# Seven block products in place of eight in the last first product of a mixer layer

## The chip, the core and the metric

One core of one Trainium2 chip runs the whole kernel as one program. The metric is the device time of one execution in microseconds. Five engines with queues of their own work side by side: PE (matrix products), DVE and ACT (elementwise work), POOL, and SP, which here only issues transfers. Each takes its instructions strictly in the order of its queue and waits there for what the instruction needs.

## What is computed

Attention inside clusters, then a channel mixing layer, then a token and channel mixer. Only the end of the last step is touched:

```python
def _moe2_ref(x, w_tok1, w_tok2, w_ch1, w_ch2):      # x: (2, 768, 512)
    xt = x.transpose(0, 2, 1)
    h = np.maximum(xt @ w_tok1, 0.0) @ w_tok2
    u = x + h.transpose(0, 2, 1)
    h2 = np.maximum(u @ w_ch1, 0.0) @ w_ch2          # w_ch1: (512, 1536), w_ch2: (1536, 512)
    return (u + h2).astype(np.float32)
```

The two products of `h2` are done one batch after the other; the change is in the first product (`u @ w_ch1`) of the second batch.

## The kernel before

**Numbers.** The weights lie in DRAM as 64-bit floats. A unit is 512 KB of them: 128 columns of `w_ch1` (all 512 rows) or 128 rows of `w_ch2`. `w_issue` (L440) starts its load into one of five staging places (`ring`); `w_split` (L450) turns it into a high and a low float32 part with five operations on DVE and two on ACT. Activations are split into the same two parts, and each product is three passes (`PASSES`): high × high, low × high, high × low.

**Units.** `c1` and `c2` are the 12 units each of the last layer. There are 14 places for converted units. `seq` is the order of loads: after the 24 units for the first batch it loads ten of them again (`CH_RELOAD`: units 4 to 0 of both kinds), since their places are given to later units in the first batch, and they are converted a second time for the second batch.

**The layer.** `ff` (L1316) goes over the 12 units of one batch. For each it does the first product in two halves of 384 rows (L1332: 4 blocks of 128 contracted channels × 3 passes = 12 matmuls of 384 columns each, into one of two PSUM banks "x" and "m"), which `act_relu` empties: ACT takes the high part (L1311), DVE the low part (L1313). Then comes the second product of the unit before (L1356: six tiles of 128 rows × 3 passes = 18 matmuls of 512 columns, summed over all units in six PSUM banks). After the last unit `finish` (L1505) adds the six banks to the input on DVE (L1508), and SP sends each out (L1509). The first batch goes through units 0 to 11, the second through 11 to 0.

**The turned input.** `Turned` (L1422) brings `u` of one batch into the form with channels on partitions: six transposes on DVE (L1437), 16 transfers on SP and POOL (L1454) and eight splits (`part`: ACT L1465, DVE L1467). `ut0` is that of the first batch, `ut1` that of the second.

**What sets the order.** The program is written out by a small planner: work on DVE, ACT and SP is made of `Chain`s, whose steps are put into the engines' queues in the order of planned times; among steps that could start within a short window the one with the earlier `due` goes first. PE's matmuls are written out by the code itself; `after` and `claim` make it wait for a chain. `later` holds chains that begin when a condition is met.

Of the kernel before, what the change touches and what calls it, by code (L numbers as in the profile page):

```python
# [9 lines left out]
F32 = mybir.dt.float32  # L10
# [293 lines left out]
def cluster_attention_moe_mixer(ctx: ExitStack, tc, q, k, v, cent, mu_k, mu_r, w_k, w_v, w_r, w1, w2, wc1, wc2, out):  # L304
# [9 lines left out]
    stk = ctx.enter_context(tc.tile_pool(name="stk", bufs=2))  # L314

# [30 lines left out]
    now = {"P": 0.0, "A": 0.0, "D": 0.0, "G": 0.0, "S": 0.0, "N": 0.0}  # L346
# [3 lines left out]
    class Chain:  # L350
# [14 lines left out]
        def step(self, n=1):  # L365
            for _ in range(n):
# [7 lines left out]
                self.ready = t + LAT  # L374
# [37 lines left out]
    units, slot_of, free_slots, staged = {}, {}, [], []  # L412
    ring = [(stg, f"raw{i}") for i in range(NSTG)]
# [8 lines left out]
    for i in range(NFC):  # L422
        seq += [("c1", i), ("c2", i)]
    for i in CH_RELOAD:
        seq += [("c1", i), ("c2", i)]
# [24 lines left out]
    def w_split():  # L450
# [5 lines left out]
        def gen():  # L456
# [16 lines left out]
            if dense[0] and seq:  # L473
                w_issue()
# [9 lines left out]
            )  # L484

# [5 lines left out]

    active, due = [], {}

    def feed():
        while staged and free_slots and staged[0][0] not in units and sum(not c.done for c in active) < 2:
            w_split()
        for wait in list(later):
# [759 lines left out]
    for n, i in enumerate(CH_RELOAD):  # L1257
        again["c1", i] = ff2 + FB * (NFC + CH_KEEP + n)
        again["c2", i] = again["c1", i] + 0.75 * FB
# [57 lines left out]
    def ff(order, ka, kb, xin, square, dropped):  # L1317
        accs, prev, chains, rls = [], None, [], []
        nf = len(order)
        for idx in range(nf + 1):  # L1320
            cur = None
            if idx < nf:
# [22 lines left out]
                cur = hl  # L1345
            if prev is not None:
                f = order[idx - 1]
                u = need((kb, f))
                for ch in chains[:2]:
# [72 lines left out]
    class Turned:  # L1422


        def __init__(self, x2, before, due):
            self.x2, self.t, self.ch, self.before, self.due = x2, None, {}, before, due
            self.added, self.main = {}, None
# [4 lines left out]
        def gen(self):  # L1432
# [12 lines left out]
            for hf in range(2):  # L1445
                for c in range(KD):
                    self.ch[hf, c] = Chain(self.part(hf, c), self.due + 4 * hf + c, now["S"] + MOVE_US)
# [11 lines left out]
        def part(self, hf, c):  # L1459
# [3 lines left out]
            src = self.u[:, :, 3 * hf : 3 * hf + 3, c, :].rearrange("p q t r -> p t q r")  # L1463
# [41 lines left out]
    def finish(b, x2, accs):  # L1505
# [5 lines left out]
        for st in range(NT):  # L1511
            banks[st] = Chain(add(st), 0.0, now["P"] + 0.2), 1

# [28 lines left out]
    ut1 = Turned(s1.x2, None, ff2 + NFC * FB - 20)  # L1542
    later.append((lambda adds=adds: all_done(adds)() and ut0.whole(), ut1.begin))
    a0 = ff(list(range(NFC)), "c1", "c2", ut0, False, CH_RELOAD)
    due.update({k: t for k, t in again.items() if k[0] in ("c1", "c2")})
    finish(0, s0.x2, a0)
    a1 = ff(list(range(NFC - 1, -1, -1)), "c1", "c2", ut1, False, list(range(NFC)))
# [38 lines left out]
```

## Time and profile before

| | us |
|---|---|
| median of 3 runs | 617.0 (615.2 to 617.99) |
| the profiled execution | 616.29 |
| its span, first to last instruction | 614.2 |
| PE busy in it | 600.9 |
| DVE busy in it | 482.2 |
| ACT busy in it | 353.3 |

Times in the trace run from the start of the span. Matmuls overlap, so the time that one costs is the distance of their starts and not the duration that a row shows. The last layer begins at 409.6 us with the first batch; the second batch begins at 509.8 us; after the last matmul, near 609.6 us, come the last adds and the last transfer.

### The profile page before, as it was taken

To read this page: it belongs to the slowest core of one execution; us is meant where nothing else is said; L and a number is where in the kernel's file an instruction comes from. 1 tells how busy PE (TensorE), PEld (TensorE's weight loads), DVE (VectorE), ACT (ScalarE), POOL (GpSimd) and SP (SyncE) were. 2 spreads that over 40 slices of the span, in tenths; PEclk is the share of its full clock that TensorE was granted. 3 is DMA by queue.
4 is the path that set the end of the run, shared out by engine and by line. 5 is a ranking of instruction groups with operands and counts; after the bars stand their busy time and mean duration, and the time that the engine had idled before them with its cause. 6 is when DMAs were issued, how large, how long until landed. Compare 5 with 4: busy or idle time off the path is not lost.

```text
span 614.2 us, 9458 instructions
## 1 busy us (share of the span) xinstructions
PE 600.9 (98%) x3309; PEld 496.0 (81%) x3309; DVE 482.2 (79%) x860; ACT 353.3 (58%) x667; POOL 122.3 (20%) x166
## 2 busy tenths in 40 slices
PE   8899999999999999999999999999999999999996
PEld 6666757657577668999899998889999989999995
DVE  6899899999899987999779889968986817784113
ACT  5888888889788667867667665134433412432100
POOL 4545743734712551000000000010002000000000
PEclk9999999999999999999999999999999999999999
DMA  8168859789647451444105343143437303300002
GB/s 289 75 186 238 233 146 259 189 255 265 176 131 198 122 168 40 139 137 132 69 1 143 131 134 107 40 98 105 148 126 172 102 1 138 125 14 0 1 1 103
DMA packets 41407, 78.84 MB, mean 128 GB/s; under 512 B 8656, under 2 KB 24016, under 8 KB 41360
## 3 DMA queue, kind: packets, MB, share of 16 engines
q1 hardware_dynamic: 38928, 70.77, 38.3%
q0 software_dynamic: 2432, 7.47, 5.1%
q8 instruction: 26, 0.43, 0.3%
q14 instruction: 21, 0.17, 0.1%
HBM read 51.42 MB, written 3.41 MB: 89 GB/s over the span
## 4 chain that ended last, share of the span: by engine, by line
PE 84%; DVE 7%; ACT 3%; DMA 2%; issue 2%; SPq 1%; POOL 1%; DVEq 0%; ACTq 0%; POOLq 0%
PE ps L1332 27%; PE ps L1356 26%; PE ps L922 10%; PE ps L839 8%; PE ps L590 5%; PE ps L906 2%; DVE junk L847 2%; ACT e L856 2%; PE ps L1412 1%; PE ps L1495 1%; PE ps L669 1%; DMA kb<-mst 1%; DMA uperm<-ublk 1%; SPq L1454 1%; DVE x L1508 1%
## 5 line engine op out<-in xcount | busy, mean ns | idle before, releaser
L1356 PE MATMUL ps<-wu,hl 128*128 128x512 f32 x720 | 170.5, 391 | 0.0
L1356 PEld LDWEIGHTS ps<-wu,hl 128*128 128x128 f32 x720 | 134.6, 188 | 26.8
L1332 PE MATMUL ps<-ut,wu 128*128 128x384 f32 x576 | 104.4, 336 | 0.1
L1332 PEld LDWEIGHTS ps<-ut,wu 128*128 128x128 f32 x576 | 101.0, 188 | 2.4 <-DVE ut L1467 0.7
L856 ACT ACTIVATE e<-ps,nm 128x768 f32<-128x768 f32 x96 | 86.5, 902 | 19.4 <-DVE junk L847 17.1
L847 DVE TENSOR_SCALAR_CACHE_REDUCE junk<-ps 128x768 bf16<-128x768 f32 x96 | 90.3, 941 | 7.4 <-PE ps L839 5.3
L1311 ACT ACTIVATE hl<-ps 128x384 fp32r<-128x384 f32 x48 | 23.4, 490 | 94.9 <-PE ps L1332 94.8
L1313 DVE SCALAR_TENSOR_TENSOR hl<-ps,hl 128x384 fp32r<-128x384 f32 x48 | 26.7, 556 | 61.1 <-ACT hl L1311 60.8
L480 ACT ACTIVATE wu<-g 128x512 fp32r<-128x512 f32 x62 | 39.1, 631 | 54.9 <-DVE g L476 54.9
L1332 PE MATMUL ps<-xmix,wu 128*128 128x384 f32 x384 | 69.2, 335 | 0.0
L1332 PEld LDWEIGHTS ps<-xmix,wu 128*128 128x128 f32 x384 | 67.3, 188 | 1.1
L839 PE MATMUL ps<-ka,qa 128*128 128x384 f32 x192 | 57.5, 381 | 1.1 <-ACT e L856 0.6
L1454 POOL DMA_DIRECT2D uperm<-ublk x16 | 7.9, 501 | 224.3 <-ACT h L1399 164.1
L839 PE MATMUL ps<-kb,qb 80*128 80x384 f32 x192 | 50.3, 344 | 1.9 <-DMA kb<-mst 1.0
L464 DVE SCALAR_TENSOR_TENSOR g<-wraw,g 128x512 uint32<-128x512 uint32 x62 | 48.1, 775 | 1.1
L482 DVE TENSOR_TENSOR wu<-g,wu 128x512 fp32r<-128x512 f32 x58 | 40.0, 690 | 8.3 <-ACT wu L480 6.8
L476 DVE SCALAR_TENSOR_TENSOR g<-wu,g 128x512 f32<-128x512 f32 x62 | 42.8, 690 | 4.5
L906 PE MATMUL ps<-ident,e 128*128 128x128 f32 x288 | 43.1, 277 | 3.0 <-ACT e L856 3.0
L885 DVE STREAM_TRANSPOSE tb<-e 128x768 f32<-128x768 f32 x48 | 45.3, 963 | 0.0
L839 PEld LDWEIGHTS ps<-ka,qa 128*128 128x128 f32 x192 | 30.2, 192 | 17.6 <-issue 7.8
L470 DVE SCALAR_TENSOR_TENSOR g<-wraw,g 128x512 uint32<-128x512 uint32 x62 | 42.4, 683 | 0.2
L906 PEld LDWEIGHTS ps<-ident,e 128*128 128x128 f32 x288 | 34.8, 142 | 7.4 <-ACT e L856 4.7
(115 smaller groups left out, 835.4 us busy)
## 6 DMA issues: line engine op xcount, KB each, us to landing
wraw<-moe_w_ch_dram SPq DMA_DIRECT2D x34, 512.0 KB, 3.2
ptd<-tb SPq DMA_DIRECT2D x88, 144.0 KB, 5.0
t<-q_dram SPq DMA_DIRECT2D x16, 384.0 KB, 5.0
t<-k_dram SPq DMA_DIRECT2D x16, 384.0 KB, 4.7
ptd<-tb POOLq DMA_DIRECT2D x40, 144.0 KB, 5.0
wraw<-moe_w_k_dram SPq DMA_DIRECT2D x9, 512.0 KB, 5.1
wraw<-moe_w_v_dram SPq DMA_DIRECT2D x9, 512.0 KB, 3.7
v<-v_dram SPq DMA_DIRECT2D x8, 384.0 KB, 3.7
```

The costliest lines, as they stand in the source:

```text
L464: nc.vector.scalar_tensor_tensor(out=g, in0=high, scalar=0xC0000000, in1=g, op0=ALU.bitwise_and, op1=ALU.bitwise_or)
L470: nc.vector.scalar_tensor_tensor(out=g, in0=low, scalar=29, in1=g, op0=ALU.logical_shift_right, op1=ALU.bitwise_or)
L476: nc.vector.scalar_tensor_tensor(out=gf, in0=f32(t[:, 1, :]), scalar=TINY, in1=gf, op0=ALU.is_ge, op1=ALU.mult)
L482: (nc.gpsimd if key[0] == "wr" else nc.vector).tensor_tensor(out=t[:, 1, :], in0=gf, in1=f32(t[:, 0, :]), op=ALU.subtract)
L839: nc.tensor.matmul(ps[:, nh, 0:HS], x[:, e, c0 : c0 + P], y[:, e, nh * HS : (nh + 1) * HS], start=first, stop=not first,)
L847: nc.vector.tensor_scalar(junk, PS_[t][:, :, 0:HS], -SCALE, None, op0=ALU.mult, op1=ALU.min, accum_out=nm)
L856: nc.scalar.activation(et.rearrange("p (a b) -> p a b", a=2), PS_.pop(t)[:, :, 0:HS], AF.Exp, bias=NM_.pop(t), scale=SCALE, accum_out=ss_[ ...
L885: nc.vector.transpose(out=T_[n][:, :, e, :, i, :].rearrange("p j k q -> p k j q"), in_=E_.pop(t).rearrange("p (k j c) -> p k j c", j=4, c=32),
L906: nc.tensor.transpose(ps[:, kk], E_[t][:, kt * P : (kt + 1) * P], ident)
L922: nc.tensor.matmul(o, vts[n][:, e, kt, :], m, start=(kt == 0), stop=(kt == NT - 1))
L1332: nc.tensor.matmul(ps[:, 0:HS], u[:, wl, c, :], xin(xl, c, sl), start=(n == 0), stop=(n == 11))
L1356: nc.tensor.matmul(accs[st], prev[:, xl, st * P : (st + 1) * P], u[:, wl, :], start=(idx == 1 and n == 0), stop=(idx == nf and n == 2),)
```

## The change

For the second batch, `ff` is replaced by a class `Seven`. It takes the units of `w_ch1` in pairs (11 and 10, 9 and 8, ...). The first product of a pair is seen as a product of 2 × 2 blocks: contracted channels in two halves, output columns by unit, rows in two halves. Seven block products (each 2 × 3 matmuls of 384 columns) with sums of weight blocks (`ssums`, four sums S per pair), of input blocks (`tsums`, `tsplit`: four sums T, once) and of results (`sum_of`, on DVE out of PSUM) give the four blocks of the result. Rounds of the second product of the pair before (`group`: 3 matmuls of 512 columns) are put between the block products; in the first pair these are the six last rounds of the first batch. The sums S lie in a buffer taken from the staging ring, which then has four places. The sums T take the place of `ut0`.

Ten converted units are written to DRAM once (`again_from`) and are loaded from there for the second batch (`w_reload`) without a second conversion. `ut1` is due 24 us earlier and leaves out two of its eight splits. The diff, cut to its core:

```diff
-    for i in CH_RELOAD:
         seq += [("c1", i), ("c2", i)]
...
-            if dense[0] and seq:
+            if wanted:
+                spare.append((ring.pop(0), wanted.clear())[0])
+            elif dense[0] and seq:
...
+            if key in again_from:
+                yield "S", 0.55, False
+                nc.sync.dma_start(out=again_from[key], in_=f32(t).rearrange("p a f -> p (a f)"))
...
+    reloads = [("c1", i) for i in CH_RELOAD] + [("c2", i) for i in CH_RELOAD]
+    again_from = {key: spill.tile([P, 1024], F32, tag=f"{key[0]}{key[1]}", name="spill") for key in reloads}
+
+    def w_reload():
+        key = reloads.pop(0)
+        pool, tag, freed = free_slots.pop(0)
+        t = pool.tile([P, 2, 512], F32R, tag=tag, name="wu")
+
+        def gen():
+            yield "R", 0.55, False
+            nc.sync.dma_start(out=f32(t).rearrange("p a f -> p (a f)"), in_=again_from[key])
+
+        units[key] = (t, Chain(gen(), due.get(key, 0.0), freed))
+        slot_of[key] = (pool, tag)
...
+        while reloads and free_slots and not staged and not seq:
+            w_reload()
...
-        again["c1", i] = ff2 + FB * (NFC + CH_KEEP + n)
-        again["c2", i] = again["c1", i] + 0.75 * FB
+        again["c1", i] = ff2 + FB * (NFC + CH_KEEP + n - 3)
+        again["c2", i] = again["c1", i] + 3.5 * FB
...
+                if hook is not None and idx == nf - 1:
+                    hook()
...
+                if hook is not None and idx == nf:
+                    def last(st):
+                        after(chains[st // HT])
+                        for n, (wl, xl) in enumerate(PASSES):
+                            nc.tensor.matmul(
+                                accs[st], prev[:, xl, st * P : (st + 1) * P], u[:, wl, :],
+                                start=False, stop=(n == 2),
+                            )
+                        spend(3 * MM512)
+                        if st == NT - 1 and f in dropped:
+                            drop((kb, f))
+                    return accs, [lambda st=st: last(st) for st in range(NT)]
...
+    class Seven:
+        def begin(self):
+            self.sums = Chain(self.tsums(), self.due - 18, now["D"])
+            later.append((lambda: spare and self.sums.done and self.units_there(0), lambda: self.begin_s(0)))
+
+        def units_there(self, q):
+            return all((self.ka, f) in units and units[self.ka, f][1].done for f in self.pairs[q])
...
+        def tsums(self):
+            x = self.xin.block
+            self.tf = []
+            for name in range(4):
+                t = temp()
...
+            t1, t2, t3, t4 = self.tf
+            for c in range(2):
+                nc.vector.tensor_tensor(out=t1[:, c], in0=x(1, c), in1=x(0, c), op=ALU.subtract)
+                nc.vector.tensor_tensor(out=t3[:, c], in0=x(1, c + 2), in1=x(1, c), op=ALU.subtract)
+                nc.vector.tensor_tensor(out=t2[:, c], in0=x(1, c + 2), in1=t1[:, c], op=ALU.subtract)
+                nc.vector.tensor_tensor(out=t4[:, c], in0=x(0, c + 2), in1=t2[:, c], op=ALU.subtract)
...
+        def begin_t(self):
+            while self.sums is None or not self.sums.done:
+                pump(None)
+            self.t = big("tt")
+            for i in (1, 2, 0, 3):
+                self.tch[i] = Chain(self.tsplit(i), self.due - 10 + i)
...
+        def tsplit(self, i):
+            src = self.tf[i].rearrange("p c t q r -> p (c t q r)")
+            yield "A", 0.77, False
+            nc.scalar.activation(self.t[i][:, 0], src, AF.Copy)
+            yield "D", 0.9, True
+            nc.vector.tensor_tensor(out=self.t[i][:, 1], in0=src, in1=f32(self.t[i][:, 0]), op=ALU.subtract)
...
+        def ssums(self, q):
+            yield "D", 0.33, True
+            w = xc.tile([P, 2, 1024], F32R, tag=f"sg{1 - q % 2}", name="ws")
+            self.st[q] = w
+            u0, u1 = (units[self.ka, f][0] for f in self.pairs[q])
+            pool, tag = spare[0]
+            sums = pool.tile([P, 1024], F32, tag=tag, name="sums")
+            full = sums.rearrange("p (i c f) -> p c i f", i=4, c=2)
+            for c in range(2):
+                if c:
+                    yield "D", 0.33, True
+                g1, g0 = (hp.tile([P, HS], F32, tag="rl", bufs=2, name="gs")[:, 0:256].rearrange("p (k f) -> p k f", k=2) for _ in range(2))
+                x0, x1 = (f32(u).rearrange("p a (k c f) -> p a c k f", k=2, c=2)[:, :, c] for u in (u0, u1))
+                nc.vector.tensor_tensor(out=g1, in0=x1[:, 0], in1=x1[:, 1], op=ALU.add)
+                yield "D", 0.33, True
+                nc.vector.tensor_tensor(out=g0, in0=x0[:, 0], in1=x0[:, 1], op=ALU.add)
+                for o, a, b, op in (
+                    (full[:, c, 0], g1[:, 0], g1[:, 1], ALU.add),
+                    (full[:, c, 1], full[:, c, 0], g0[:, 0], ALU.subtract),
+                    (full[:, c, 2], g0[:, 0], g1[:, 0], ALU.subtract),
+                    (full[:, c, 3], g0[:, 1], full[:, c, 1], ALU.subtract),
+                ):
+                    yield "D", 0.2, True
+                    nc.vector.tensor_tensor(out=o, in0=a, in1=b, op=op)
...
+            for i in range(2):
+                sl = slice(i * 512, (i + 1) * 512)
+                yield "A", 0.55, False
+                nc.scalar.activation(w[:, 0, sl], sums[:, sl], AF.Copy)
+                yield "D", 0.62, True
+                nc.vector.tensor_tensor(out=w[:, 1, sl], in0=sums[:, sl], in1=f32(w[:, 0, sl]), op=ALU.subtract)
...
+            def group():
+                q, k, st = queue.pop(0)
+                if q is None:
+                    k()
+                    before.append(finish_one(st))
+                    return
+                f = self.pairs[q][k]
+                u = need((self.kb, f))
+                after(done[q, k, st // HT])
+                if st not in accs:
+                    accs[st] = acc_bank(st, "acc")
+                left[st] -= 1
+                for n, (wl, xl) in enumerate(PASSES):
+                    nc.tensor.matmul(
+                        accs[st], self.hl[q][k][:, xl, st * P : (st + 1) * P], u[:, wl, :],
+                        start=(left[st] == 2 * np_ - 1 and n == 0), stop=(left[st] == 0 and n == 2),
+                    )
+                spend(3 * MM512)
...
+            def product(ps, a, b):
+                n = 0
+                for c in range(2):
+                    for wl, xl in PASSES:
+                        nc.tensor.matmul(ps[:, 0:HS], a(wl, c), b(xl, c), start=(n == 0), stop=(n == 5))
+                        n += 1
+                    spend(3 * MM384)
...
+                if q % 2 == 0:
+                    hl = [hp.tile([P, 2, S], F32R, tag="hl", name="hl")]
+                else:
+                    for ch in before:
+                        ch.force()
+                    t = xb.tile([P, 2, 2, S], F32R, tag="x0", name="hl")
+                    hl = [t[:, 0], t[:, 1]]
+                self.hl[q] = hl
...
+                def sum_of(out, ps, other):
+                    yield "D", 0.48, False
+                    nc.vector.tensor_tensor(out=out, in0=ps[:, 0:HS], in1=other, op=ALU.add)
+
+                def split(c, k, sl):
+                    yield "A", 0.4, False, 1.0
+                    nc.scalar.activation(hl[k][:, 0, sl], c, AF.Relu)
+                    yield "D", 0.48, True
+                    nc.vector.scalar_tensor_tensor(
+                        out=hl[k][:, 1, sl], in0=c, scalar=0.0, in1=f32(hl[k][:, 0, sl]), op0=ALU.max, op1=ALU.subtract
...
+                def second(ps):
+                    yield from sum_of(c11, ps, p1)
+                    yield from split(c11, 0, lo_h)
+
+                def third(ps):
+                    yield from sum_of(c21, ps, u3)
+                    yield from split(c21, 1, lo_h)
+
+                def fourth(ps):
+                    yield from sum_of(u4, ps, u2)
+                    yield from sum_of(c22, ps, u3)
+                    yield from split(c22, 1, hi_h)
+
+                def fifth(ps):
+                    yield from sum_of(c12, ps, u4)
+                    yield from split(c12, 0, hi_h)
...
+                turn[0] ^= 1
+                px, tx = small_bank("h")
+                product(px, a11, b11)
+                ch1 = chain(copy1(px), tx, 1)
+                pm, tm = small_bank("h")
+                product(pm, s(1), t(1))
+                ch1.force()
+                ch2 = chain(sum_of(u2, pm, p1), tm, 1)
+                groups(2 if q == 0 else 3)
+                claim(tx)
+                product(px, a12, b21)
+                done[q, 0, 0] = chain(second(px), tx, 1)
+                groups(2 if q == 0 else 1)
+                claim(tm)
+                ch2.force()
+                product(pm, s(2), t(2))
+                ch3 = chain(sum_of(u3, pm, u2), tm, 1)
+                groups(2)
+                claim(tx)
+                product(px, a22, t(3))
+                ch3.force()
+                if q % 2 == 0:
+                    hl.append(hp.tile([P, 2, S], F32R, tag="hl", name="hl"))
+                done[q, 1, 0] = chain(third(px), tx, 1)
+                groups(2)
+                claim(tm)
+                product(pm, s(0), t(0))
+                done[q, 1, 1] = ch5 = chain(fourth(pm), tm, 2)
+                groups(2)
+                claim(tx)
+                product(px, s(3), b22)
+                ch5.force(1)
+                done[q, 0, 1] = chain(fifth(px), tx, 1)
+                groups(9)
+                drop((self.ka, f0)), drop((self.ka, f1))
...
+                if q + 2 < np_:
+                    later.append((lambda q=q: q + 1 in self.sch and self.sch[q + 1].done and self.units_there(q + 2), lambda q=q: self.begin_s(q + 2)))
+                queue += [(q, 0, st) for st in range(HT)] + [(q, 1, st) for st in range(NT)] + [(q, 0, st) for st in range(HT, NT)]
...
-    ut1 = Turned(s1.x2, None, ff2 + NFC * FB - 20)
+    ut1 = Turned(s1.x2, None, ff2 + NFC * FB - 44, False)
     later.append((lambda adds=adds: all_done(adds)() and ut0.whole(), ut1.begin))
-    a0 = ff(list(range(NFC)), "c1", "c2", ut0, False, CH_RELOAD)
+    seven = Seven(list(range(NFC - 1, -1, -1)), "c1", "c2", ut1, ff2 + NFC * FB, 2 * FB - 6 * MM384)
+    wanted.append(True)
+    later.append((ut1.whole, seven.begin))
+    later.append((lambda: 0 in seven.sch and seven.sch[0].done and seven.units_there(1), lambda: seven.begin_s(1)))
+    a0, last0 = ff(list(range(NFC)), "c1", "c2", ut0, False, CH_RELOAD, seven.begin_t)
     due.update({k: t for k, t in again.items() if k[0] in ("c1", "c2")})
-    finish(0, s0.x2, a0)
-    a1 = ff(list(range(NFC - 1, -1, -1)), "c1", "c2", ut1, False, list(range(NFC)))
+    a1 = seven.run(last0, lambda st: finish(0, s0.x2, a0, st), list(range(NFC)))
```

## Rows read from the trace of the kernel before

**Rows 1.** The page's first part: busy us (share of span) x instructions, by engine.
```profile
PE 600.9 (98%) x3309; PEld 496.0 (81%) x3309; DVE 482.2 (79%) x860; ACT 353.3 (58%) x667; POOL 122.3 (20%) x166
```
**Rows 2.** Stretches: length; busy PE, PEld, DVE, ACT, POOL (x instructions); granted clock; DMA share, GB/s.
```profile
440.00:489.00 49.00, 49.00 (x249) 44.58 (x248) 40.38 (x73) 20.03 (x39) 3.91 (x8) 1.00 0.48 135
489.00:505.50 16.50, 16.50 (x86) 15.02 (x84) 2.76 (x6) 1.97 (x4) 0.00 (x0) 1.00 0.04 14
...
560.00:609.60 49.60, 49.58 (x246) 44.12 (x244) 9.51 (x16) 5.29 (x11) 0.00 (x0) 1.00 0.04 14
```
**Rows 3.** The chain that ended last, from 560 us: start, us, what.
```profile
563.97 4.18 PE ps L1332 x24
568.15 4.12 PE ps L1356 x18
...
606.22 4.09 DVE x L1508 x6
```
**Rows 4.** Timeline: PE where the batches meet (start, us, what, count).
```profile
501.60 8.36 PE L1356 MATMUL ps<-wu,hl 128*128 128x512 f32 x36
...
509.81 8.51 PE L1332 MATMUL ps<-ut,wu 128*128 128x384 f32 x48
```
**Rows 5.** Groups by line and shape, whole span: count, busy us, mean ns, idle before.
```profile
L482 DVE TENSOR_TENSOR wu<-g,wu 128x512 fp32r<-128x512 f32 x58 | 40.0, 690 | 8.3 <-ACT wu L480 6.8
L1313 DVE SCALAR_TENSOR_TENSOR hl<-ps,hl 128x384 fp32r<-128x384 f32 x48 | 26.7, 556 | 61.1 <-ACT hl L1311 60.8
L544 DVE TENSOR_TENSOR xmix<-t,xmix 128x768 fp32r<-128x768 f32 x8 | 7.6, 956 | 0.3 <-ACT xmix L542 0.2
...
L965 DVE COPY cn<-ps 128x128 f32<-128x128 f32 x1 | 0.3, 293 | 0.4 <-PE ps L958 0.4
...
L542 ACT ACTIVATE xmix<-t 128x768 fp32r<-128x768 f32 x16 | 13.4, 842 | 12.3 <-DVE t L535 12.1
```
**Rows 6.** Timeline: DVE operations that follow each other, six of 512, five of 384 columns.
```profile
376.55 3.67 DVE L1381 TENSOR_TENSOR x<-ps,sg 128x512 f32<-128x512 f32 x6
...
410.68 2.42 DVE L1467 TENSOR_TENSOR ut<-uperm,ut 128x384 fp32r<-128x384 f32 x5
```
**Rows 7.** Timeline: first and last step of the second batch's ten conversions (50 DVE steps).
```profile
515.19 0.42 DVE L460 TENSOR_SCALAR g<-wraw 128x512 uint32<-128x512 uint32 x1
...
558.91 0.69 DVE L482 TENSOR_TENSOR wu<-g,wu 128x512 fp32r<-128x512 f32 x1
```
**Rows 8.** Timeline: one unit's matmuls, and ACT's reading of its first half.
```profile
580.42 4.35 PE L1332 MATMUL ps<-ut,wu 128*128 128x384 f32 x24
582.72 0.49 ACT L1311 ACTIVATE hl<-ps 128x384 fp32r<-128x384 f32 x1 [5.73 <-PE ps L1332]
```
**Rows 9.** Transfers after 400 us: issues, KB each, median us from issue to landing.
```profile
wraw<-moe_w_ch_dram SPq DMA_DIRECT2D x21, 512.0 KB, 3.3
out_dram<-x SPq DMA_DIRECT2D x12, 256.0 KB, 2.1
```
**Rows 10.** Timeline: the second batch's turned input is split, and the bank readers behind it.
```profile
474.61 3.43 ACT L1465 ACTIVATE ut<-uperm 128x384 fp32r<-128x384 f32 x8 [5.02 <-DMA wraw<-moe_w_ch_dram]
475.17 3.84 DVE L1467 TENSOR_TENSOR ut<-uperm,ut 128x384 fp32r<-128x384 f32 x8 [3.92 <-ACT ut L1465]
...
479.00 0.56 DVE L1313 SCALAR_TENSOR_TENSOR hl<-ps,hl 128x384 fp32r<-128x384 f32 x1
...
480.81 4.35 PE L1332 MATMUL ps<-ut,wu 128*128 128x384 f32 x24
```
**Rows 11.** Timeline: the first batch's turned input, its transfers and PE's waits.
```profile
397.76 5.49 SPq L1454 DMA_DIRECT2D uperm<-ublk  x8
...
400.21 0.69 DVE L482 TENSOR_TENSOR wu<-g,wu 128x512 fp32r<-128x512 f32 x1 [0.70 <-ACT wu L480]
...
407.38 3.42 ACT L1465 ACTIVATE ut<-uperm 128x384 fp32r<-128x384 f32 x8 [5.11 <-DMA uperm<-ublk]
...
411.28 2.58 PEld L1332 LDWEIGHTS ps<-ut,wu 128*128 128x128 f32 x15 [0.45 <-DVE ut L1467]
```

More of the change, by code (lines that the diff above doesn't have):

```diff
@@ L314, in cluster_attention_moe_mixer @@
     stk = ctx.enter_context(tc.tile_pool(name="stk", bufs=2))
+    spill = ctx.enter_context(tc.tile_pool(name="spill", bufs=1, space=bass.MemoryType.DRAM))
     ident = const.tile([P, P], F32, name="ident")
@@ L343, in late_constants @@
             nc.gpsimd.memset(t[:, :, 0:1], 0.0)
-    now = {"P": 0.0, "A": 0.0, "D": 0.0, "G": 0.0, "S": 0.0, "N": 0.0}
+    now = {"P": 0.0, "A": 0.0, "D": 0.0, "G": 0.0, "S": 0.0, "N": 0.0, "R": 0.0}
     lock = [0.0, 0.0]
@@ L373, in step @@
                     lock[0] = t
-                self.ready = t + LAT
+                self.ready = t + (RAW_US if e == "R" else LAT)
                 self.count += 1
@@ L412, in cluster_attention_moe_mixer @@
     units, slot_of, free_slots, staged = {}, {}, [], []
+    spare, wanted = [], []
     ring = [(stg, f"raw{i}") for i in range(NSTG)]
@@ L1315, in act_relu, with ff @@
         )
-    def ff(order, ka, kb, xin, square, dropped):
+    def ff(order, ka, kb, xin, square, dropped, hook=None):
         accs, prev, chains, rls = [], None, [], []
@@ L1422, in cluster_attention_moe_mixer, with __init__ @@
     class Turned:
-        def __init__(self, x2, before, due):
+        def __init__(self, x2, before, due, whole=True):
             self.x2, self.t, self.ch, self.before, self.due = x2, None, {}, before, due
+            self.parts = [(hf, c) for hf in range(2) for c in range(KD) if whole or (hf, c // 2) != (1, 0)]
             self.added, self.main = {}, None
@@ L1444, in gen, with block @@
                     self.move(g, qi), self.move(g, qi + 1)
-            for hf in range(2):
-                for c in range(KD):
-                    self.ch[hf, c] = Chain(self.part(hf, c), self.due + 4 * hf + c, now["S"] + MOVE_US)
+            for hf, c in self.parts:
+                self.ch[hf, c] = Chain(self.part(hf, c), self.due + 4 * hf + c, now["S"] + MOVE_US)
+        def block(self, hf, c):
+            return self.u[:, :, 3 * hf : 3 * hf + 3, c, :].rearrange("p q t r -> p t q r")
         def move(self, g, qi):
@@ L1462, in part @@
                 self.t = big("ut")
-            src = self.u[:, :, 3 * hf : 3 * hf + 3, c, :].rearrange("p q t r -> p t q r")
+            src = self.block(hf, c)
             h, l = (self.view(part, hf)[:, c, :].rearrange("p (t q r) -> p t q r", t=HT, q=4) for part in range(2))
@@ L1503, in mixer, with finish @@
         return adds
-    def finish(b, x2, accs):
+    def finish(b, x2, accs, only=None):
         def add(st):
```

62 lines of the change are left out of this document (60 added, 2 removed).

## The prediction

> **What bounds the kernel now.** I read the table of busy shares first [rows 1]: TensorE (PE) is busy for 600.9 of 614.2 us, DVE for 79%, ACT for 58%. A share over the whole span decides nothing, so the next view is the busy time by stretches [rows 2]. From 440 us to 609.6 us PE is busy in every stretch, at full granted clock: nothing but PE's own work can be shortened there. DVE has room, but not evenly: 40.38 of 49 us from 440 to 489, then 2.76 of 16.5, and 9.51 of 49.6 in the last stretch. Last comes the chain that ended last [rows 3]: the end is matmuls of the first product (24 in 4.18 us) and of the second (18 in 4.12 us) in turn, without a gap, then the six last adds. The matmul starts of [rows 4] give the stage: the last stretch of the first batch, 36 matmuls of the second product, starts at 501.60 (505.7 at its half), the second batch at 509.81. So a matmul removed after 440 us is time removed, unless a wait takes its place.
>
> **What is removed.** The first product of the second batch is 12 units of 24 matmuls, 288 in all. By pairs it is 7 products of 6 matmuls, 42 where 48 stood, so 6 × 6 = 36 fewer. A matmul of 384 columns costs 4.18 / 24 = 0.174 us [rows 3], and 36 cost **6.27 us**. The 216 matmuls of the second product stay, at 0.229 us each. Rounds of three of them are now put between the block products; at the old changes between the two kinds the next matmul starts in its turn (4.18 + 4.12 = 8.30 us, the period of the chain), so I cost more changes at nothing.
>
> **What is added for DVE and ACT.** Durations are those of [rows 5]: 0.556 us for 384 columns, 0.69 for 512, and 0.956 for 768. What an operation takes from a busy queue is less, by [rows 6]: six of 512 take 3.67 us, one each (3.67 − 0.69) / 5 = 0.60; five of 384 take 2.42, one each 0.47; so 0.13 us for 128 columns and 0.08 fixed. Operations of 256 and of 128 columns are in no row of this stage; by the line they take 0.34 and 0.21 us of the queue and last 0.42 and 0.29 (a copy of 128 lasted 0.293 in [rows 5]). I take the queue's numbers, since DVE's operations here follow each other; the durations are the upper end.
> Once, ahead of the second batch: T sums, 8 of 384, 3.7 us; T splits, 4 of 768, about 3.5 us (ACT 4 × 0.84); two parts of the turned input fall away, 0.9 us.
> Each pair: weight sums, 4 × 0.34 + 8 × 0.21 + 2 × 0.60 = 4.2 us (5.4 by durations); seven sums out of the banks, 3.3 us; four splits as before, 1.9. Together **9.4 us of a pair's 42 × 0.174 + 36 × 0.229 = 15.55 us** (11.5 by durations). ACT gets three operations more, none longer than the 0.84 us of 768 columns, and is the emptier engine of the two [rows 1]. Ten weight conversions of 3.2 us DVE, which stand from 515 to 559 in the trace before [rows 7], go.
>
> **The waits, step by step.** There are still two banks, px and pm, for seven products of 1.04 us. Each must be read before it is written again. From the trace, ACT starts 0.2 us after the last matmul [rows 8], so a sum is done some 0.8 us after its product if DVE is free. Writing the pair's order as a time line of PE, the next use of its bank comes 3.1, 3.8, 3.1, 3.8, 3.8, 3.8 and 2.4 us after the end of the first to seventh product (the last is the tightest, with 1.6 us to spare). So in pairs two to six I cost the waits at nothing: rounds of the previous pair's second product hide them.
> The first pair is different: its queue holds only the six last rounds of the first batch, gone before the fourth product. The last three products stand bare. c21 is done some 0.8 us after the fourth, within the fifth product's 1.04 us; but the fifth feeds two sums and the next pair's first product wants its bank: 0.2 + 0.47 + 0.56 against 1.04, plus a split in between. I take **0.4 us**, between 0 and 2.
> T and the start: T overwrites the first batch's turned input, free once its last first product ends (501.6). The first T split takes 0.2 + 0.84 + 0.96, done near 503.7; it is wanted at 505.7 + 1.04 = 506.7. Hidden by the last round but one of the second product, and 2 us late at worst if two other operations stand ahead.
> DRAM: a load of 512 KB lands in 3.3 us, a write of 256 KB in 2.1 [rows 9]. The ten writes follow the conversions of units 0 to 4 early in the first batch (one of these ends near 401 [rows 11]); a reload is first wanted by the weight sums of the fourth pair, a whole pair after its slot is free. Hidden; a write that SP must hold until DVE's last step is done delays the weight loads behind it, and these run several units ahead. Cover gone, a late reload would cost up to its 3.3 us.
> The staging ring has one place fewer and the second batch's input is turned some 24 us earlier: 0 to 1 us; I take 0.3 for it.
> Sum: 614.2 − 6.27 + 0.4 + 0.3 = 608.6 us of span. The profiled execution took 616.29, 2.1 more than its span, so 610.7; it lay 0.7 under the median of 617.0. **Forecast 611.4 us.**
>
> **A rule against it.** Back-to-back rows show a fixed 0.08 us for each DVE operation in the queue [rows 6]. [...] The change cuts weights into pieces of 128 and 256. [...]
>
> **Rivals.**
> A. The forecast, 610 to 613: chance 0.66.
> B. DVE is the bound around the first pair. From 489 to the second pair's start (near 517) it has 28 us. By the queue's numbers it needs 2.8 (what stands there) + 3.7 + 3.5 (T) + 8.4 (two weight sums) + 3.6 (six adds of the first batch) + 5.1 (seven sums, four splits) = 27.1; by durations 32. Against: 8.6 us are free between 440 and 489, so T sums can go ahead. For: 3.9 us of those are a wait for the turned input [rows 10]. If it decides, some 4 us: 615.4. It decides when the first weight sum is not done by 506.7. Chance 0.15.
> C. The input's move. Turned earlier, the split of the second batch's input stands in DVE's and ACT's queues and waits for its DMAs: 5.02 us of ACT and 3.92 of DVE in the trace before, and the banks' readers behind it ended 1.25 us before PE wanted the bank (479.56 against 480.81) [rows 10]. A move that lands 3 us later, behind one 512 KB write, gives PE a wait of about 2 us: 613.4. The first batch's own moves, near 398 to 403 us, have the conversion at 400.21 and its write beside them, and there PE already waits for the split input [rows 11]: the same price. Chance 0.10.
> D. Slower: weight sums get ahead of a bank's sum in DVE's strict order. From 1.6 us of backlog on the last product's bank is late; with a whole weight sum of 4.2 ahead, PE waits 2.6 us in each of five pairs, 13 us against 6.3 gained: 624. For: 14 operations of a weight sum in every pair; against: DVE is needed for 9.4 of 15.55 us and sums are due at once. Half of it is no gain. Chance 0.07.
> E. The matmuls go, but changes between products and rounds cost PE 0.07 us each, 14 in a pair and six pairs: nothing is gained, 617. Against: today's changes cost nothing [rows 3]. Chance 0.02.
>
> **How the numbers follow.** What a measurement of this kernel can tell from no change is about 0.5%, 3.1 us. A is faster; B falls to no change in most of its weight, C is faster; D is slower, E no change. Faster 0.66 + 0.10 + a little of B = 0.77, same 0.15, slower 0.08. Low end: the whole 6.27 without any wait gives 610.7, less the 1.8 us by which a run lay under the median: 609.0. The high end takes in B: 615.5. D and E lie outside.
>
> **What would show it.** In the profile after: 252 matmuls of 384 columns in the second batch, in groups of 6 of 1.04 us; first of them near 505.7 and last matmul near 603.3; pair period 15.55 us; PE without idle time from pair two on; weight sums and bank sums on DVE at about 60% of the last 90 us; no conversions in the second batch; ten writes and ten loads of 512 KB. B would show as PE waiting for DVE between 506 and 518, C as a wait near 410 or 450 to 480, D as the same wait in every pair. Wrong in the whole would be a pair period over 16.6 us.

## The result, and the profile after

The changed kernel takes 609.37 us (median of five runs), the kernel before 617.09 us in the same comparison; over the runs of both, the ratio is 0.9884, with a 95% interval of 0.9854 to 0.9914. A sixth run of the changed kernel took 657.44 us at a granted clock of 0.85 and is left out; with it the median is 609.72, the figure that an expectation below uses. A second comparison gave 609.68 against 615.95, 0.9904 (0.9880 to 0.9928). Both are faster by more than 0.5%. The forecast was 611.4, its range 609.0 to 615.5; the profiled execution has a span of 608.3 us, where the sum gave 608.6.

The first part of the page and the busy time of three pairs (columns as in [rows 2]) stand against [rows 1, 2]:

```profile
PE 595.6 (98%) x3273; PEld 489.9 (81%) x3273; DVE 506.2 (83%) x946; ACT 354.2 (58%) x667; POOL 123.1 (20%) x166
```
```profile
533.20:548.90 15.70, 15.70 (x80) 14.14 (x79) 10.41 (x26) 3.75 (x7) 0.00 (x0) 1.00 0.40 132
548.90:564.60 15.70, 15.70 (x80) 14.11 (x79) 10.38 (x26) 3.74 (x7) 0.00 (x0) 1.00 0.29 103
564.60:580.20 15.60, 15.60 (x79) 14.10 (x78) 10.31 (x26) 3.75 (x7) 0.00 (x0) 1.00 0.01 2
```

3273 matmuls stand where 3309 stood: 36 fewer. PE is still busy in all of each pair, and DVE in two thirds of it. The chain that ended last (start, us, what) is PE again, now product and rounds in turn, where [rows 3] had 24 and 18:

```profile
533.39 2.08 PE ps L1666 x12
535.48 2.06 PE ps L1654 x9
537.53 1.06 PE ps L1666 x6
538.60 0.70 PE ps L1654 x3
539.29 1.05 PE ps L1666 x6
540.35 1.37 PE ps L1654 x6
541.72 1.06 PE ps L1666 x6
...
549.05 1.04 PE ps L1666 x6
```

Two products without a change between them take 2.08 us (0.1733 a matmul); one behind a round takes 1.06, not 1.04. From 533.39 to 549.05 it is one pair: 15.66 us, where the sum had 15.55.

The spans of the two traces of the kernel before differ by 1.6 us, and what lies ahead of its last layer differs by as much: the third unit of the first batch begins at 422.66 us in one and at 420.91 in the other. So all kernels are compared between two points: the start of the first product of that unit and the end of PE's last matmul. These are the two rows of the trace before, then of the trace after:

```profile
422.66 4.35 PE L1332 MATMUL ps<-ut,wu 128*128 128x384 f32 x24
...
601.22 8.36 PE L1356 MATMUL ps<-wu,hl 128*128 128x512 f32 x36
```
```profile
422.65 4.35 PE L1354 MATMUL ps<-ut,wu 128*128 128x384 f32 x24
...
594.52 9.79 PE L1654 MATMUL ps<-wu,hl 128*128 128x512 f32 x42
```

| kernel | between the two points, us | against the changed kernel | from there to the end of the span |
|---|---|---|---|
| before (two traces) | 186.92, 187.13 | +5.26, +5.46 | 4.62, 4.56 |
| after (two traces) | 181.66, 181.67 | 0 | 3.99, 3.94 |
| e1_eight | 187.92 | +6.26 | 3.95 |
| e2_reload_only | 186.92 | +5.26 | 4.00 |
| e3_convert_again | 192.92 | +11.26 | 4.13 |
| e4a_dve6 | 181.66 | 0 | 4.03 |
| e4b_dve14 | 191.99 | +10.33 | 3.99 |
| e5_move_early | 185.39 | +3.73 | 3.95 |
| e6_spread | 181.36 | −0.30 | 4.00 |
| e7_bare | 181.84 | +0.18 | 3.94 |

(Each is worked out from such a pair of rows; for the kernel before 601.22 + 8.36 − 422.66. The two traces of the kernel before differ by 0.21 us between the points, those of the kernel after by 0.01. e4a_dve6, e4b_dve14, e5_move_early and e7_bare are one execution each.)

### The profile page after: what moved, and what is told of

It is laid out like the page before. It is cut to its first block, busy times and chain, and to the rows that moved or that the text cites. A ratio compares the mean times of both kernels' runs of the same rounds, so it can differ in the third digit from the quotient of the medians.

```text
span 608.3 us, 9503 instructions
## 1 busy us (share of the span) xinstructions
PE 595.6 (98%) x3273; PEld 489.9 (81%) x3273; DVE 506.2 (83%) x946; ACT 354.2 (58%) x667; POOL 123.1 (20%) x166
## 4 chain that ended last, share of the span: by engine, by line
PE 83%; DVE 7%; DMA 4%; ACT 3%; issue 2%; SPq 1%; DVEq 0%; ACTq 0%
PE ps L1354 19%; PE ps L1392 18%; PE ps L944 9%; PE ps L861 8%; PE ps L1654 8%; PE ps L1666 7%; PE ps L612 5%; PE ps L928 3%; DVE junk L869 2%; DMA t<-k_dram 2%; ACT e L878 2%; PE ps L1448 1%; PE ps L1534 1%; PE ps L691 1%; DMA kb<-mst 1%
## 5 line engine op out<-in xcount | busy, mean ns | idle before, releaser
L1392 PEld LDWEIGHTS ps<-wu,hl 128*128 128x128 f32 x486 | 90.8, 188 | 18.0
L482 ACT ACTIVATE wu<-g 128x512 fp32r<-128x512 f32 x52 | 32.8, 631 | 43.7 <-DVE g L478 43.6
L1354 PE MATMUL ps<-ut,wu 128*128 128x384 f32 x288 | 52.5, 336 | 0.5 <-DVE ut L1506 0.5
L1354 PEld LDWEIGHTS ps<-ut,wu 128*128 128x128 f32 x288 | 50.5, 188 | 1.9 <-DVE ut L1506 1.0
L1654 PEld LDWEIGHTS ps<-wu,hl 128*128 128x128 f32 x216 | 40.2, 188 | 6.6
L1713 ACT ACTIVATE hl<-t 128x384 fp32r<-128x384 f32 x24 | 12.6, 525 | 55.1 <-DVE t L1709 55.1
L464 DVE SCALAR_TENSOR_TENSOR g<-wraw,g 128x512 uint32<-128x512 uint32 x52 | 41.2, 792 | 1.0
L1709 DVE TENSOR_TENSOR t<-ps,t 128x384 f32<-128x384 f32 x42 | 22.8, 555 | 21.1 <-PE ps L1666 20.0
L478 DVE SCALAR_TENSOR_TENSOR g<-wu,g 128x512 f32<-128x512 f32 x52 | 35.9, 689 | 3.6
```

The source lines that it names most:

```text
L464: nc.vector.scalar_tensor_tensor(out=g, in0=high, scalar=0xC0000000, in1=g, op0=ALU.bitwise_and, op1=ALU.bitwise_or)
L478: nc.vector.scalar_tensor_tensor(out=gf, in0=f32(t[:, 1, :]), scalar=TINY, in1=gf, op0=ALU.is_ge, op1=ALU.mult)
L1354: nc.tensor.matmul(ps[:, 0:HS], u[:, wl, c, :], xin(xl, c, sl), start=(n == 0), stop=(n == 11))
L1392: nc.tensor.matmul(accs[st], prev[:, xl, st * P : (st + 1) * P], u[:, wl, :], start=(idx == 1 and n == 0), stop=(idx == nf and n == 2),)
L1654: nc.tensor.matmul(accs[st], self.hl[q][k][:, xl, st * P : (st + 1) * P], u[:, wl, :], start=(left[st] == 2 * np_ - 1 and n == 0), stop=(l ...
```

## The experiments

**Eight products in the new order.**

```diff
                 product(px, a11, b11)
+                product(px, a11, b11)
```


> The changed kernel, in which the first block product of each pair is done twice (the second overwrites the first), so that eight products of 6 matmuls stand where seven stood; everything else of the change stays. Theory 1 (the gain is the 36 matmuls, 36 x 0.174 = 6.27 us, and nothing else): the span goes back by 6.2 us, from 608.3 to about 614.5, near that of the kernel before; pair period 15.66 + 1.04 = 16.70 us. Rival (the gain comes from the ten conversions that fell away, or from rounds and products in turn): the span stays within 2 us of 608.3.

Measured: +6.26 us between the points; 615.56 us by the clock, 0.9983 of before (0.9964 to 1.0002). The twelve matmuls stand together in the timeline, and the next pair's stand 16.72 us behind (550.51 to 567.23):

```profile
550.51 2.25 PE L1666 MATMUL ps<-ut,wu 128*128 128x384 f32 x12
...
567.23 2.25 PE L1666 MATMUL ps<-ut,wu 128*128 128x384 f32 x12
```

It follows that the gain is the 36 matmuls: 6.26 measured, 6.27 in the sum. What is left against the kernel before between the points (187.92 against 186.92) is 1.0 us that the new order costs. By the clock this kernel is 1.1 us faster than the one before, where the points, the shorter end and the time around the span make it some 0.2 us slower; the interval reaches 0.1 us slower, and what is left of the difference lies ahead of the first point, where no run isolates it.

**Only the DRAM copies.**

```diff
-    for i in CH_RELOAD:
-        seq += [("c1", i), ("c2", i)]
...
+            if key in again_from:
+                yield "S", 0.55, False
+                nc.sync.dma_start(out=again_from[key], in_=f32(t).rearrange("p a f -> p (a f)"))
...
+        while reloads and free_slots and not staged and not seq:
+            w_reload()
```


> The kernel before, with nothing of the seven products: only the ten converted units are written to DRAM and loaded again, in place of a second load and conversion. Theory 1 (PE bounds both batches of this layer; conversions and their DMAs were hidden): no change, 614 us of span within 1 us. Rival (the DRAM copies brought a part of the gain): 2 us or more faster than before.

Measured: 186.92 us between the points, the same as before to 0.01:

```profile
422.28 4.35 PE L1352 MATMUL ps<-ut,wu 128*128 128x384 f32 x24
...
600.84 8.36 PE L1376 MATMUL ps<-wu,hl 128*128 128x512 f32 x36
```

By the clock it is 615.38 against 616.7, 0.9975 (0.9958 to 0.9992): some 1.3 us less (0.5 to 2.6), outside the points. Of it 0.6 is at the end (last section). So the ten conversions that fell away were free: PE bounds the stage with them or without.

**Seven products without the DRAM copies.**

```diff
+    seq += [("c1", i) for i in CH_RELOAD] + [("c2", i) for i in CH_RELOAD]
...
-            if key in again_from:
-                yield "S", 0.55, False
-                nc.sync.dma_start(out=again_from[key], in_=f32(t).rearrange("p a f -> p (a f)"))
...
-        while reloads and free_slots and not staged and not seq:
-            w_reload()
```


> The changed kernel with seven products, but the ten units are loaded as raw weights and converted a second time, as before; no DRAM copies. Theory 1 (the DRAM copies bring nothing by themselves but make room on DVE for the weight sums): DVE needs 9.4 us a pair and 32 us for the conversions, 69.6 us in the four pairs of 62.6 us in which places come free, so the weight sums come late and PE waits some 5 to 8 us: span 613 to 616, PE waiting for ws or wu in pairs three to five. Rival (DVE has room enough, the copies were not needed): 608.3 within 1 us.

Measured: +11.26 us, 619.5 us by the clock, 1.0045 of the kernel before (1.0024 to 1.0066). PE's waits, and the stretches around them (columns as in [rows 2]; the eighth is the granted clock):

```profile
574.70 1.95 PE L1650 MATMUL ps<-wu,hl 128*128 128x512 f32 x3 [3.07 <-ACT wu L483]
...
593.13 0.51 PE L1650 MATMUL ps<-wu,hl 128*128 128x512 f32 x1 [2.78 <-ACT wu L483]
```
```profile
571.00:574.70 3.70, 0.63 (x5) 0.31 (x3) 3.50 (x7) 1.21 (x3) 0.00 (x0) 0.88 0.48 155
574.70:578.40 3.70, 3.70 (x10) 3.06 (x11) 2.23 (x5) 0.55 (x1) 0.00 (x0) 0.50 0.42 133
578.40:582.00 3.60, 3.60 (x14) 3.07 (x13) 1.83 (x6) 0.00 (x0) 0.00 (x0) 0.69 0.00 0
589.00:593.10 4.10, 1.36 (x8) 1.03 (x6) 3.71 (x7) 2.23 (x4) 0.00 (x0) 1.00 0.01 2
593.10:596.00 2.90, 2.64 (x7) 1.91 (x8) 2.52 (x5) 1.20 (x2) 0.00 (x0) 0.70 0.00 0
596.00:600.00 4.00, 4.00 (x18) 3.59 (x17) 2.11 (x5) 0.53 (x1) 0.00 (x0) 0.79 0.00 0
```

PE waits for a weight that is still being converted, while DVE is busy in 3.50 of 3.70 us. The waits add up to 6.1 us (3.07 + 2.74 + 0.26 from these rows), within the 5 to 8 expected, though they stand in pairs five and six and not three to five; the span of 621.4 us is far over the 613 to 616 expected. Most of the other 5 us is PE's clock. It falls in the first wait (0.88 over the stretch that holds it) and is 0.50 behind it, where six matmuls of 384 columns last 2.12 us (at 576.44) and not the 1.21 at 1.00 (at 566.26). Four stretches at 0.50, 0.69, 0.70 and 0.79 cost 1.85 + 1.12 + 0.79 + 0.84 = 4.6 us, each worked out as PE's busy time in it by what its clock lacks to 1.00. So the copies bring nothing between the points by themselves, and beside the seven products 11.26 us. One thing is not shown: this kernel converts all five units of `w_ch1` ahead of the five of `w_ch2`, for which PE then waits; the kernel before takes them in turn. What seven products cost with that order no run tells.

**More work for DVE.** Additions whose result is not used:

```diff
+            for _ in range(6 if q > 1 else 0):
+                yield "D", 0.6, True
+                g = cvt.tile([P, 512], U32, tag="g", name="g")
+                nc.vector.tensor_tensor(out=f32(g), in0=sums[:, 0:512], in1=sums[:, 512:1024], op=ALU.add)
```


> The changed kernel with six more DVE additions of 512 columns (into a scratch tile, not used) behind the weight sums of pairs three to six: 3.6 us more in each of four pairs. Theory 1 (DVE is needed for 9.4 of 15.66 us of a pair, 6.2 are free): 13.0 of 15.66, pair period unchanged within 0.3 us, span within 1 us of 608.3. Rival (DVE's strict order already makes bank sums late): PE waits in these pairs, 1 us or more for each, span over 612.

With 14 in place of 6:

> The same with fourteen more additions, 8.4 us in each of four pairs. Theory 1 (6.2 us are free): 17.8 of 15.66 us, so DVE becomes the bound and four pairs lose about 2.1 us each, less the lead that the weight sums have: span 612 to 617, pair period near 17.8 us. If DVE had more room than the queue's numbers say (another theory): span under 610. By durations in place of distances (11.5 of 15.66 needed) the loss would be 4.2 us a pair: span over 622.

Measured: six cost nothing (181.66 us between the points). Fourteen cost 10.33 us, more than forecast (span 619.6, not 612 to 617), and now a bank sum is what PE waits for, in each of the four pairs (0.97 us in the last, not shown). A pair takes 18.37 us (542.16 to 560.53), with DVE busy in 18.07 of 18.30:

```profile
542.16 1.32 PE L1671 MATMUL ps<-tt,ws 128*128 128x384 f32 x6 [1.86 <-DVE t L1714]
560.53 1.32 PE L1671 MATMUL ps<-tt,ws 128*128 128x384 f32 x6 [2.42 <-DVE t L1714]
578.90 1.72 PE L1671 MATMUL ps<-tt,ws 128*128 128x384 f32 x6 [2.44 <-DVE t L1714]
```
```profile
542.20:560.50 18.30, 15.91 (x78) 14.01 (x78) 18.07 (x40) 3.64 (x7) 0.00 (x0) 1.00 0.34 116
```

Behind the third of these waits the clock fell to 0.67 for 5.1 us, 1.7 of the 10.33 us; the period is taken ahead of it, at 1.00. So a pair needs 18.37 − 14 × 0.60 = 10.0 us of DVE, not the 9.4 of the queue's numbers and not the 11.5 of durations; 5.7 us are free. That and the clock make up the miss. Rival D is real as a mechanism and lies more than 3.6 us of added work away.

**The turned input's splits too early.**

```diff
-                self.ch[hf, c] = Chain(self.part(hf, c), self.due + 4 * hf + c, now["S"] + MOVE_US)
+                self.ch[hf, c] = Chain(self.part(hf, c), self.due + 4 * hf + c, now["S"] + (MOVE_US if len(self.parts) == 8 else 0.0))
```


> The changed kernel, but the splits of the second batch's turned input are put into the queues as if its transfers landed at once, 3.7 us earlier than planned. Theory 1 (the wait for these transfers, 5.64 us of ACT and 4.87 of DVE, costs PE nothing because the bank readers behind it end 0.84 us before PE wants the bank): the wait grows to about 9 us and PE loses what exceeds the margin, 2 to 3 us: span 610.5 to 611.5, with PE waiting near 450 us. Rival (the order of ACT and DVE goes round it, bank readers are not behind it): no change within 0.5 us.

Measured: +3.73 us. In the changed kernel the wait is there and free; this is its timeline, with the answer to [rows 10]:

```profile
451.89 2.18 ACT L1504 ACTIVATE ut<-uperm 128x384 fp32r<-128x384 f32 x5 [5.64 <-DMA uperm<-ublk]
452.44 1.97 DVE L1506 TENSOR_TENSOR ut<-uperm,ut 128x384 fp32r<-128x384 f32 x4 [4.87 <-ACT ut L1504]
...
454.48 0.56 DVE L1335 SCALAR_TENSOR_TENSOR hl<-ps,hl 128x384 fp32r<-128x384 f32 x1
...
455.88 4.35 PE L1354 MATMUL ps<-ut,wu 128*128 128x384 f32 x24
```

And this is the experiment's:

```profile
451.48 2.59 ACT L1504 ACTIVATE ut<-uperm 128x384 fp32r<-128x384 f32 x6 [7.93 <-DMA wraw<-moe_w_ch_dram]
...
456.72 0.55 DVE L1335 SCALAR_TENSOR_TENSOR hl<-ps,hl 128x384 fp32r<-128x384 f32 x1
...
457.32 2.93 PE L1354 MATMUL ps<-ut,wu 128*128 128x384 f32 x11 [1.88 <-DVE hl L1335]
```

The reader of the first bank ends 0.84 us ahead of PE in the one and holds PE up in the other, for 2.0 us (455.3 to 457.3). That was expected; the rest of the 3.73 was not, and it is PE's clock again:

```profile
457.30:460.00 2.70, 2.67 (x11) 2.68 (x12) 2.66 (x5) 0.00 (x0) 0.00 (x0) 0.72 0.00 0
460.00:463.00 3.00, 3.00 (x13) 3.00 (x13) 2.88 (x5) 0.88 (x2) 0.00 (x0) 0.68 0.58 177
```

At 0.72 and 0.68 these stretches lose 0.76 + 0.96 = 1.7 us. Rival C's mechanism is right; here it had 0.84 us to spare, and beyond that this wait of 2.0 us cost 3.7.

**Other places for the rounds of the first pair.**

```diff
-                groups(2)
+                groups(1 if q == 0 else 2)
...
-                groups(2)
+                groups(0 if q == 0 else 2)
...
-                groups(2)
+                groups(1 if q == 0 else 2)
```


> The changed kernel with the six rounds of the first pair laid out as 2, 2, 1, 0, 1 after the second to sixth product, in place of 2, 2, 2, 0, 0. Theory 1 (the wait of PE before the second pair, 0.39 us on its weight load, is the missing cover behind the fifth block product, whose two sums must both be read): that wait goes, span 0.3 to 0.5 us shorter, 607.9. Rival (DVE is full in the first pair and only moves the wait): PE waits at another product of pairs one or two, span 608.3 or more.

Measured: −0.30 us between the points; by the clock 610.25 us, 0.9884 of before (0.9859 to 0.9908), which can't be told from the changed kernel. The changed kernel at the end of its first pair: the product that feeds two sums, a product behind it, the two sums, and the next product held by them.

```profile
515.12 1.20 PE L1666 MATMUL ps<-tt,ws 128*128 128x384 f32 x6
516.16 1.21 PE L1666 MATMUL ps<-ut,ws 128*128 128x384 f32 x6
516.36 1.02 DVE L1709 TENSOR_TENSOR t<-ps,t 128x384 f32<-128x384 f32 x2 [0.48 <-PE ps L1666]
...
517.44 1.00 PEld L1666 LDWEIGHTS ps<-ut,wu 128*128 128x128 f32 x6 [0.39 <-DVE t L1709]
```

In the experiment the same two products stand at 514.78 and 515.84 without a wait:

```profile
513.04 1.20 PE L1666 MATMUL ps<-tt,ws 128*128 128x384 f32 x6
...
514.08 0.86 PE L1377 MATMUL ps<-wu,hl 128*128 128x512 f32 x3
...
514.78 1.22 PE L1666 MATMUL ps<-ut,ws 128*128 128x384 f32 x6
...
515.84 1.20 PE L1666 MATMUL ps<-ut,wu 128*128 128x384 f32 x6
```

**No rounds between the products, from the second pair on.**

```diff
-                groups(2 if q == 0 else 3)
+                groups(2 if q == 0 else 0)
...
-                groups(9)
+                groups(9 if q == 0 else 12)
```

(and 0 for the other places in these pairs)

> The changed kernel, but in pairs two to six all twelve rounds of the second product come behind the seven block products, none between them. Theory 1 (rounds between the products hide the reading of the banks; a product of 1.04 us alone covers one sum of about 0.8 us but not two sums, or a sum behind other work of DVE): PE waits 0.4 to 1 us in each of five pairs as it did in the first, span 610.5 to 613.5. Rival (one product covers the reading of the other bank, the rounds were not needed): span 608.3 within 0.5 us.

Measured: +0.18 us, no more than the two traces of the kernel before differ by. The rival has it from the third pair on: pairs three to five take 15.56 to 15.62 us, where the changed kernel takes 15.66 to 15.68. PE waits between the products only in the second pair, where a bank sum stands behind weight sums, and that pair takes 16.37 us and not 15.79:

```profile
520.05 0.55 DVE L1709 TENSOR_TENSOR t<-ps,t 128x384 f32<-128x384 f32 x1
...
520.66 1.33 PE L1666 MATMUL ps<-tt,ws 128*128 128x384 f32 x6 [0.36 <-DVE t L1709]
```

One product of 1.04 us covers the reading of the other bank by one sum (0.2 + 0.56). Only the bank with two sums needs more, and behind its successor stand the twelve rounds anyhow.

**Both kernels again.** The same two programs, each with a second trace:

> The kernel before, once more, with a trace of its own. Counted from the first product of the third unit in the first batch (422.66 us in the trace before) to PE's last matmul it took 186.92 us, and 4.62 us from there to the end. Theory 1 (the gain between these two points is the whole effect; what lies ahead of them and behind them differs from run to run): 186.9 again, an end of 4.0 us as in six other traces or of 4.6. Rival (the order of the last transfers makes the end 0.6 us longer in this kernel): 4.6 us again.

> The changed kernel, once more, with a trace of its own, beside the kernel before on the same chip. Theory 1: 181.66 us between the same two points, 4.0 us behind them, and a time 5.3 to 6 us shorter than that of the kernel before on this chip. Rival (a further gain of 1 to 2 us, as in the first comparison of 617.09 with 609.72, is the change's own): 7 us or more shorter, with a part ahead of the first point that is shorter than before by 1 us in both traces.

Measured: 187.13 and 181.67 between the points, 4.56 and 3.94 behind them. The rival of the first has its 0.6 us at the end again, but the order of the last transfers is not its cause: the kernel with DRAM copies alone has the old order and 4.00 us. In the second, 609.68 against 615.95 is 6.27 us on one chip, between the two forecasts, and the part ahead of the first point is not shorter in both traces (420.91 before, 422.39 after). The first comparison, by its ratio 7.2 us with an interval of 5.3 to 9.0, is no evidence of more than that; the traces account for 5.3 to 5.5 + 0.6 at the end + 0.1 around the span (1.93 to 1.8 us on average), 6.0 to 6.2 in all.

## Why the prediction was right, point by point

- **What is removed.** 6.27 us forecast, 6.26 measured by putting the matmuls back (e1_eight).
- **What bounds the stage.** PE alone: without the conversions nothing changed (e2_reload_only), and six more DVE operations a pair changed nothing (e4a_dve6).
- **Changes between products and rounds at nothing.** This term was mis-sized. A product behind a round takes 1.06 us and not 1.04, five or so times a pair: 15.66 against 15.55 us, 0.55 in five pairs. The row of the old period hid it: 4.18 us for 24 matmuls already held one such change, 24 × 0.1733 = 4.16. Rival E was this at 0.07 for each of 14 changes a pair; 15.66 − 42 × 0.1733 − 36 × 0.229 = 0.14 us over as many makes it 0.01. e7_bare bears it out: with two changes left in a pair, pairs three to five take 15.56 to 15.62 us.
- **The first pair.** 0.4 us forecast for the bank with two sums, 0.39 us of waiting in the trace, gone where a round covers it (e6_spread, −0.30). The split that the forecast allowed for did not come between: the two sums stand back to back. In the order of the code it is the sixth product that feeds two sums; where the prediction speaks of the first pair's fourth and fifth product, and the expectation of e6_spread of the fifth, each is one further on.
- **Rounds hide the waits.** Right in the result and too strong as a reason: without rounds pairs three to six still don't wait (e7_bare). A product is cover enough, as the prediction's own 0.8 against 1.04 us says.
- **Start of the second batch.** Nothing was late. The first weight sums ended at 495.8 and were wanted at 506.8; the T sums went ahead of them, from 471.5 to 476.7. Rival B had 11 us to spare, not none: the 8.6 us free ahead of 489 were what it left out of its sum. The 0.3 us set down for the ring and the earlier turning was nothing too: the second batch's first product begins at 505.72 in the trace after, and 501.60 + 18 × 0.229 = 505.72 is where the trace before puts that point. Nor did PE lose anything at rival C's other place, near 411 us, where the first batch's turned input has a DRAM write beside it: its weight loads go on at 411.27 us after and at 411.28 before.
- **DVE's need.** 9.4 us forecast by distances, 11.5 by durations, 10.0 measured with a full queue (e4b_dve14). The weight sums themselves are as estimated: 0.34 us for 256 columns and 0.20 to 0.21 for 128 from start to start, 0.31 where an operation reads the result of the one before:

```profile
488.63 0.41 DVE L1616 TENSOR_TENSOR gs<-wu 128x256 f32<-128x256 f32 x1
488.97 0.41 DVE L1618 TENSOR_TENSOR gs<-wu 128x256 f32<-128x256 f32 x1
489.31 0.28 DVE L1626 TENSOR_TENSOR sums<-gs 128x128 f32<-128x128 f32 x1
489.62 0.29 DVE L1626 TENSOR_TENSOR sums<-sums,gs 128x128 f32<-128x128 f32 x1
489.83 0.28 DVE L1626 TENSOR_TENSOR sums<-gs 128x128 f32<-128x128 f32 x1
```

  The rows last 0.41 and 0.28 to 0.29 us, where the prediction's durations were 0.42 and 0.29. As a price in a queue the measured distances decide, and they are 17 to 29% lower (0.34 against 0.41, 0.20 against 0.28).
- **DRAM.** A reload lands 4.4 us after its issue (median of the ten), not the 3.3 of the loads in the trace before; no wait of PE for one stands in the trace after. The ten writes go out from 354.9 to 424.3 us, most of them ahead of this layer.
- **The end.** 0.6 us shorter, not forecast (next section but one). With it the sum is 614.2 − 6.26 + 0.39 + 0.55 − 0.6 = 608.3. That 608.6 came so close is in part luck: 0.55 too little for the changes stands against 0.3 too much for the start and 0.6 for the end. Without the end it shows: the last matmul ends at 604.3 us, where 609.6 − 6.27 + 0.7 puts it at 604.0 (the 603.3 among the prediction's signs leaves its own waits out).
- **From span to median.** The forecast added 0.7 us because the profiled execution of before lay that far under its median. The one of after lay 0.70 over its own (610.07 against 609.37). That turn of 1.4 us, 0.3 us of span and 0.3 us less around the span are the 2.0 us between 611.4 and 609.4.

## What to carry to other kernels

Here, where PE was busy without a gap and at a granted clock of 1.00, a matmul taken out was worth its distance to the next (36 × 0.174 = 6.27 us forecast, 6.26 measured), and the question was only whether the sums that replace it fit beside: count the other engine's need per period from distances of starts, leave room over that (10.0 us a pair measured here, 9.4 counted), and ask what must be cleared away first. Here the seven products with the conversions left in, in the order of e3_convert_again, made the kernel slower (619.5 us, 1.0045 of before), and moving ten conversions to DRAM alone gave nothing between the points (186.92 us in both). Two banks were enough here for products of 1.04 us where each was read once and DVE was free for it; the bank that two operations read needed one more piece of work between (0.39 us of waiting without it, none with it).

## What the runs showed of the hardware that was not expected

PE's clock made some waits dearer than they look. In steps of half a microsecond the traces of the kernels before and after show a granted clock of 1.00 or, from 28.5 to 31.5 us, of 0.50, with a figure between only beside these (0.84 from 28.0 to 28.5 us and 0.75 from 31.5 to 32.0 before, 0.59 from 31.5 to 32.0 after); the longer stretches with a figure between are taken to hold both. Behind a wait of 3.07 us the granted clock was 0.50 for the next 3.7 us (e3_convert_again, whose two waits cost 6.1 us of waiting and 4.6 of slow matmuls; it fell while PE still waited, 0.88 on average from 571.0 to 574.7 us); behind one of 2.0 us it was 0.72 and 0.68 for 5.7 us (e5_move_early), and behind one of 2.44 us 0.67 for 5.1 (e4b_dve14). It is not every time: in e4b_dve14 the waits of 1.86 and 2.42 us were followed by 1.00. What tells these cases apart the runs don't show.

The end of the kernel differs by 0.6 us, and not through the seven products: e1_eight, with eight, and e2_reload_only, with nothing but the copies, have the short end too. From the transfers of the last 10 us, first of the kernel before, then of the one after:

```profile
DMA packets 865, 1.58 MB, mean 155 GB/s; under 512 B 96, under 2 KB 96, under 8 KB 864
q14 instruction: 1, 0.01, 0.2%
```
```profile
DMA packets 864, 1.57 MB, mean 169 GB/s; under 512 B 96, under 2 KB 96, under 8 KB 864
```

One packet of instructions falls among the last six output transfers of the kernel before, in both of its traces, and the slowest of these lands 2.5 us behind its issue; in the kernel after and in the one with DRAM copies alone there is no such packet and the slowest takes 2.1 to 2.2. The three traces of kernels that convert the ten units a second time (two of the kernel before, one of e3_convert_again) have the packet; two of the kernel after and one of e2_reload_only, all with DRAM copies, don't, and the nine traces with DRAM copies have an end of 3.94 to 4.03 us. So the short end seems to come with that part of the change. In e3_convert_again the packet falls among the first three of the six transfers, one of which takes 2.6 us, and its end is 4.13 us. The six are issued in two threes there, within 5.83 us, and in the kernel before without a gap, within 3.73. That fits a packet that delays the transfers it falls among, and an end that grows only where no gap follows; but no run moved the packet alone, so that it is the cause is argued and not shown. What makes up the rest of the 1.3 us by which e2_reload_only was faster by the clock stays open; 0.6 us lies within its interval.
